# Batch 0 in tiles of 128 queries, k in the layout of q, v in one set of loads, and a new order, in a fused cosine-attention and highway kernel

## The chip, the core and the metric

The kernel runs on one core of a Trainium2 chip. A core has five engines that run side by side and meet at semaphores: TensorE (PE; its weight loads are listed as PEld), VectorE (DVE), ScalarE (ACT), GpSimd (POOL) and SyncE (SP), and 16 DMA engines. DMAs that SP and ACT issue go through hardware queues; those of POOL go through a software queue and can change the type on the way (fp32 to fp16 here). The metric is the device time of one execution in microseconds; lower is better. The kernel before took 270.19 us (median of three runs, 269.24 to 270.47).

## What is computed

```python
# q, k, v: (8, 12, 448, 64) fp32: batch, heads, sequence, head dimension; tau = 0.1
q_n = q / (norm(q) + 1e-6);  k_n = k / (norm(k) + 1e-6)
scores = q_n @ k_n.T / tau                     # no mask
attn = softmax(scores);  y = attn @ v
x = y.transpose(0, 2, 1, 3).reshape(3584, 768) # heads side by side
H = relu(x @ w_h);  T = sigmoid(x @ w_t + b_t) # w_h, w_t: (768, 768)
out = T * H + (1 - T) * x                      # (3584, 768) fp32
```

So each of the 8 batches has an attention of 12 heads, and then a highway layer over its 448 rows; here the latter is called the FFN.

## The kernel before, in words

**Tiling.** A row of the sequence is l * 7 + j, with l from 0 to 63 and j from 0 to 6. Heads are taken in three *quads* (g = 0, 1, 2) of four heads, two *pairs* each (s = 0, 1); pair p of batch b has number n = 6b + p. The two heads of a pair (t = 0, 1) lie in the upper and lower half of TensorE's rows. q has partition (s, l) and 7 x 64 values of a row set; it is normalised to `qn`, turned by seven transposes a quad into `Tq` and copied to `qT`. k has another layout before: 384 of the 448 keys as three chunks of 128 (`kr`, or for batch 0 fp32 pieces in the `os` buffers), the last 64 keys of each head apart as *tails* (`kt`, with a block-diagonal `kb`). v is split in the same way (`vr`, `vt`, and `vp`, which holds it with a column of ones).

**Steps of a batch.** Squares of q and k on ACT (`norm_q`, `norm_k`, `norm_t`: lines L368, L388, L391, L402), sums on DVE (L376, L397, L404), the reciprocal root by two Newton steps in seven short DVE instructions (`newton`, L416 to L423), scaling on POOL (`scale_q` L434, `scale_k` L495, `scale_kb` L502; for the first quad partly on DVE), transposes on PE (L446, L460, L465) and copies out of PSUM on DVE (L451, L471 to L475). For each pair then six score matmuls in three row-paired groups (`scores`, L531) and one for the tails (L542), 448 queries wide, each followed by an exp on ACT (L537, L544): seven exps a pair. `attend` makes the product with v (L556, L561, L569), a reciprocal (L576) and the scaling into `x` (L577). `ffn(b, i)` has four tiles a batch (i = 0 to 2 with two j each, i = 3 with the last): transposes of x (L600), a copy (L602), products with `wt` and `wh` (L616, L613), `za` adds the bias (L625), tanh on ACT (L632), `gt`, `hm`, `gg` on DVE (L634, L628, L637), `out` on POOL or DVE (L642), and the store `st` on SP. `x` of a batch is one token: FFN tile 0 of batch 0 waits for all six pairs.

**Order.** No loop sets the order. Every step is registered as an operation with a sequence number (`pl.op`), and the tuple `ORDER` lists these numbers in the order in which they are emitted; each engine and each DMA queue works through its own in that order. `SLOTS` gives each use of a ring (a set of buffers) its buffer. `PORT` names the kinds of DVE and POOL operations between which an ordering wait is added. 18 matmuls on zeros (`wm`, L279) run first on PE.

**The start.** SP loads quad 0 of q (448 KB) and ACT the first sixth of k (192 KB), SP then the tails, the other sixths, the other quads. POOL clears `vp` (L266), loads v in halves, then k and v of batch 1 (L309, L327), later `wt` and `wh` (L335). The bias comes on SP behind q of batch 2.

Of the kernel before, what the change touches and what calls it, by code (L numbers as in the profile page):

```python
# [8 lines left out]
FP32 = mybir.dt.float32  # L9
# [120 lines left out]
}  # L130


PORT = ("nt", "gt", "gg", "vc", "qn", "kn", "kb", "vt", "out")


class Op:
# [65 lines left out]
def kernel(  # L202
# [11 lines left out]
    nc = tc.nc  # L214
# [555 lines left out]
```

## Time and profile before

| | us |
|---|---|
| median of three runs | 270.19 |
| the profiled execution | 270.06 |
| its span, first to last instruction | 268.3 |
| PE busy | 251.6 |
| DVE busy | 233.4 |
| ACT busy | 214.5 |
| POOL busy | 169.8 |

The 1.76 us between the execution's time and its span lie outside the instructions. A view by windows gives, for each stretch, the busy time of each engine with its number of instructions, the clock that TensorE was granted (1.00 is full speed), the mean share of the DMA engines' time (over 1 where transfers overlap on one engine) and the rate. A row of the timeline or of the chain of waits begins with its start and its length in us. In a row of groups, the number after "x" is the count, then come busy time and the mean length in ns. Matmuls overlap in the pipeline and their ends are modelled, so that a "busy" PE can still be held up by a producer: how much PE does is read from counts.

### The profile page before, as it was taken

How to read it: one execution, taken by the hardware profiler on the slowest of the kernel's cores; microseconds unless marked ns; L12 is line 12 of the kernel's file. 1: busy time of each engine (PE TensorE's matmuls, PEld its weight loads, DVE VectorE, ACT ScalarE, POOL GpSimd, SP SyncE). 2: the span in 40 equal slices, each digit the busy share in tenths (PEclk: the TensorE clock that was granted, in tenths of full speed). 3: DMA queues.
4: the chain of work that ended last, by engine and by line, in shares of the span. 5: the costliest groups of instructions: out<-in, count | busy, mean ns of one | idle time of the engine just before them, and what ended most of it. 6: DMA issues, size and time to landing. Idle time of an engine off the chain costs nothing.

```text
span 268.3 us, 7687 instructions
## 1 busy us (share of the span) xinstructions
PE 251.6 (94%) x3042; PEld 158.8 (59%) x3042; DVE 233.4 (87%) x523; ACT 214.5 (80%) x421; POOL 169.8 (63%) x212
## 2 busy tenths in 40 slices
PE   8375999999999999999999999999999999999990
PEld 2122566656756576657656685666666675667660
DVE  2987988799999999999989899999998788657993
ACT  3389899999589997999899996999979757883120
POOL 6467878306975679668957397659555686320650
PEclk9755799999999999999999999999999999999998
DMA  7999999999307990496995972990513101052146
GB/s 173 298 290 181 208 270 261 213 255 126 44 18 221 234 182 14 146 257 159 151 142 185 164 107 67 330 135 4 147 23 100 29 15 49 0 147 65 29 135 190
DMA packets 51092, 38.64 MB, mean 144 GB/s; under 512 B 37488, under 2 KB 47856, under 8 KB 51056
## 3 DMA queue, kind: packets, MB, share of 16 engines
q1 hardware_dynamic: 25888, 26.75, 36.2%
q0 software_dynamic: 24896, 11.21, 33.1%
q8 instruction: 24, 0.39, 0.5%
q10 hardware_dynamic: 272, 0.20, 0.2%
q14 instruction: 12, 0.10, 0.1%
HBM read 38.34 MB, written 11.01 MB: 184 GB/s over the span
## 4 chain that ended last, share of the span: by engine, by line
PE 81%; DMA 6%; DVE 4%; ACT 4%; SPq 1%; issue 1%; POOL 1%; ACTq 0%; DVEq 0%
PE B L616 33%; PE B L531 12%; PE B L561 10%; PE B L613 5%; DMA os<-in_k_dram 4%; PE B L556 4%; PE B L600 4%; PE B L446 3%; PE B L542 3%; PE B L569 3%; PE B L460 3%; ACT E L537 3%; DMA out_dram<-os 1%; PE B L465 1%; DVE hm L628 1%
## 5 line engine op out<-in xcount | busy, mean ns | idle before, releaser
L537 ACT ACTIVATE E<-B 128x448 f16<-128x448 f32 x288 | 137.4, 577 | 15.6 <-PE B L531 12.6
L642 POOL TENSOR_TENSOR os<-x,hm 128x384 f32<-128x384 f16 x53 | 47.5, 911 | 50.2 <-DVE hm L637 39.6
L616 PEld LDWEIGHTS <-xT 128*128 128x128 f16 x576 | 51.2, 98 | 34.8 <-issue 7.5
L434 POOL TENSOR_TENSOR qn<-qr,y 128x448 f16<-128x448 f32 x47 | 43.4, 934 | 24.6 <-issue 8.1
L616 PE MATMUL B<-wh,xT 128*128 128x384 f16 x288 | 57.6, 326 | 0.0
L616 PE MATMUL B<-wt,xT 128*128 128x384 f16 x288 | 56.7, 326 | 0.0
L531 PE MATMUL B<-qT,kT 64*128 64x448 f16 x288 | 43.5, 367 | 2.8 <-DVE kT L473 1.5
L561 PE MATMUL B<-vp,E 128*128 128x65 f16 x864 | 44.5, 195 | 0.0
L561 PEld LDWEIGHTS <-E 128*128 128x128 f16 x864 | 39.1, 99 | 2.9
L632 ACT ACTIVATE tt<-z 128x768 f16<-128x768 f32 (+1 forms) x32 | 25.3, 793 | 18.5 <-DVE z L625 14.8
L495 POOL TENSOR_TENSOR kp<-kr,y 128x384 f16<-128x384 f16 x42 | 34.3, 827 | 8.2 <-DVE tt L634 2.6
L628 DVE SCALAR_TENSOR_TENSOR hm<-B,x 128x384 f16<-128x384 f32 x56 | 30.5, 549 | 3.0 <-PE B L616 1.7
L556 PE MATMUL B<-vp,Et 128*128 128x130 f16 x144 | 32.3, 224 | 0.0
L625 DVE TENSOR_TENSOR z<-B,bias 128x384 f32<-128x384 f32 x48 | 25.9, 551 | 6.5 <-PE B L616 5.5
L544 ACT ACTIVATE Et<-B 128x448 f16<-128x448 f32 x48 | 27.9, 597 | 3.1 <-PE B L542 2.8
L577 DVE SCALAR_TENSOR_TENSOR x<-B,rd 128x448 f16<-128x448 f32 x48 | 29.2, 617 | 0.6
L376 DVE TENSOR_REDUCE n<-sq 128x14 f32<-128x896 f32 (+1 forms) x25 | 25.8, 1040 | 1.2 <-ACT sq L368 1.2
L397 DVE TENSOR_REDUCE n<-sq 128x18 f32<-128x1152 f32 (+2 forms) x17 | 21.5, 1269 | 4.2 <-ACT sq L388 3.8
L368 ACT ACTIVATE sq<-qr 128x896 f32<-128x896 f32 (+1 forms) x24 | 23.1, 978 | 1.1 <-DMA qr<-in_q_dram 1.1
L531 PEld LDWEIGHTS <-kT 64*128 64x128 f16 x288 | 10.3, 94 | 20.1 <-issue 12.3
L556 PEld LDWEIGHTS <-Et 128*128 128x128 f16 x144 | 14.1, 98 | 7.9 <-issue 4.7
L542 PE MATMUL B<-qT,kT 128*128 128x448 f16 x48 | 17.4, 371 | 1.1 <-DVE kT L475 1.1
(59 smaller groups left out, 363.3 us busy)
## 6 DMA issues: line engine op xcount, KB each, us to landing
qr<-in_q_dram SPq DMA_DIRECT2D x7, 1344.0 KB, 7.6
out_dram<-os SPq DMA_DIRECT2D x48, 192.0 KB, 3.3
kr<-in_k_dram POOLq DMA_DIRECT2D x7, 576.0 KB, 12.2
vr<-in_v_dram POOLq DMA_DIRECT2D x7, 576.0 KB, 10.3
kt<-in_k_dram SPq DMA_DIRECT2D x16, 96.0 KB, 6.4
vt<-in_v_dram SPq DMA_DIRECT2D x16, 96.0 KB, 7.5
out_dram<-os SPq DMA_DIRECT2D x16, 96.0 KB, 2.9
qr<-in_q_dram SPq DMA_DIRECT2D x3, 448.0 KB, 6.9
```

The costliest lines, as they stand in the source:

```text
L434: ENG[eng].tensor_mul(R("qn", 3 * b + g)[:, :, t, :], R("qr", b)[:, g + 3 * t, :].rearrange("l (j d) -> l j d", d=D), R("y", b)[:, c : c + ...
L495: ENG[eng].tensor_mul(R("kp", 6 * b + p).rearrange("l c t d -> l t c d"), a, kcol(b, p))
L531: nc.tensor.matmul(R("B", ("S", n, c, t))[:, 0:S], lhsT=R("kT", i)[ln, s, 128 * c : 128 * c + 128], rhs=R("qT", i)[ln, s, :], start=True, ...
L537: nc.scalar.activation(R("E", n)[:, at : at + 7, :].rearrange("l j x -> l (j x)"), R("B", ("S", n, c, t))[:, 0:S], AF.Exp)
L544: op("ACT", f"expt {n}", lambda: nc.scalar.activation(R("Et", n).rearrange("l j x -> l (j x)"), R("B", ("St", n))[:, 0:S], AF.Exp), r=[("B ...
L556: nc.tensor.matmul(U[:, 2 * c : 2 * c + 2, :], lhsT=Et[:, 2 * c : 2 * c + 2, :].rearrange("l j x -> l (j x)"), rhs=vp[:, 6:8, 0:65], start ...
L561: nc.tensor.matmul(U[:, 2 * c + t, :], lhsT=E[:, at : at + 2, :].rearrange("l j x -> l (j x)"), rhs=vp[:, 3 * t + m, 0:65], start=False, s ...
L577: op("DVE", f"ev {n}", lambda: nc.vector.scalar_tensor_tensor(out=R("x", b)[:, :, D * p : D * p + D], in0=U_()[:, :, 0:D], scalar=0.0, in1 ...
L616: nc.tensor.matmul(P[:, 0:MH], lhsT=xT[:, cc, :], rhs=w_[:, cc, MH * mh : MH * mh + MH], start=(cc == 0), stop=(cc == CC - 1))
L625: op("DVE", f"za {g} {mh}", lambda at=at, sl=sl: nc.vector.tensor_add(R("z", g)[:, sl], R("B", at)[:, 0:MH], biast[:, :] if tail else bias ...
L628: op("DVE", f"hm {g} {mh}", lambda at=at, sl=sl, mh=mh: nc.vector.scalar_tensor_tensor(out=R("hm", g)[:, sl], in0=R("B", at)[:, 0:MH], sca ...
L642: op(eng, f"out {g} {mh}", lambda sl=sl, mh=mh: ENG[eng].tensor_add(R("os", g)[:, sl], xpart(mh), R("hm", g)[:, sl]), r=[("gg", g), ("x", ...
```

## The change

The queries of batch 0 are worked in four tiles like those of the FFN: `attend0(g, i)` does, for quad g, 128 queries (64 for i = 3), writes `x` as tokens `("x", 0, i)`, and FFN tile i of batch 0 needs only its own. Its scores are 128 (64) columns wide, the tails' scores share a bank with those of t = 0, and one exp of 512 and one of 384 columns do what seven of 448 did for a quarter of the queries. Batches 1 to 7 keep `scores` and `attend`.

k takes the layout of q, for all batches: one load, squares and sums of 896 columns a quad, `kn` with eight slots of two heads (the first and last half zero), eight transposes a quad, one copy. The tails' loads, squares, sums and scalings go. k of batch 0 comes in fp32 by hardware queues, a quad at a time, into the `E` buffers; it must be scaled before exps can use the buffer. v comes in four loads a batch on POOL, its tails among them; SP's loads of tails go. The Newton steps of batch 0 are replaced by ln and exp on ACT (`lnexp`), which need another activation table: one is loaded at the start, and a second one (`table2`) after the last `lnexp`. The clearing of `vp` moves from POOL to DVE, ahead of the zeros for the matmuls. Loads of q for batches 1 and up are *held* on SP until the ACT instruction ahead of them in the order has ended. qT and kT have four buffers instead of three, xT five instead of three.

With the numbers of the new `ORDER` resolved to operations, the queues begin as follows (batch, quad, half):

```
SP   q 0 0; k 0 1; q 0 1; q 0 2; k 0 2; (held) q 1 0; q 1 1; q 1 2; bias; (held) q 2; q 3; st 1; ...
POOL load k 1; ident; four loads v 0; load wt; load wh; kn 0 0 1; qn 0 0 1; load k 2; qn 0 1; kn 0 1; kn 0 2 1; qn 0 2; ...
ACT  load k 0 0; table; sq q 0 0 (one half); sq k 0 0 (two halves); ln, exp; sq k 0 1; sq q 0 1; sq q 0 2; ln, exp;
     sq k 0 2; two exps; sq k 1 0; ln; exp tile; exp; three exps; sq q 1 0; table2; 20 exps, 18 of them of tiles 0 and 1; ...
DVE  vp; zeros; ... sq q 0 0 (other half); four sums; kn 0 0 0; qn 0 0 0; sum k 0 1; zeros of kn 0; sum q 0 1; copy kT 0; copy qT 0; ...
PE   18 x wm; turn k 0 0; turn q 0 0; scores of quad 0, tiles 0 and 1; turn q 0 1; turn k 0 1; ...
```

On PE, the FFN of batch 0 stands among the scores and products of batch 0's tiles 1 to 3 and of batch 1. As before, its last part (tile 3) and the last product of batch 1 (pair 11) stand right ahead of the turn of q of batch 2.

The diff, cut:

```diff
-    WARM = 18
+    WARM, NF = 18, 0
+    XDMA = ()
+    GROUPS = ((0, 1), (1, 2), (2, 3)), ((0, 1), (1, 3)), ((0, 3),)
+    LG = ((0, 0), (0, 28), (0, 56))
+    SCALE = {("q", 0, 0): ("DVE", "POOL"), ("k", 0, 0): ("DVE", "POOL")}
...
+        self.held = eng == "SP" and kind == "ldq" and name.split()[1] != "0"
...
+    def ld_kf(g, eng):
+        op(eng, f"ldf {g}", lambda: ENG[eng].dma_start(kf(g), q_src(k, 0)[:, :, g::3, :]), w=[("E", ("f", g))])
+    def ld_v(b):
+        for t, jj, j0, n in ((0, 0, 0, 4), (0, 1, 4, 3), (1, 0, 0, 3), (1, 1, 3, 4)):
+            def fn(t=t, jj=jj, j0=j0, n=n):
+                c = 64 if (t, jj) == (0, 1) else 0
+                nc.gpsimd.dma_start(R("vr", b)[64 * jj : 64 * jj + 64, 6 * t : 6 * t + 6, c : c + 64 * n].rearrange("l h (c d) -> l h c d", c=n),
+                                    v_src(b)[:, 6 * t : 6 * t + 6, j0 : j0 + n, :])
+            op("POOL", f"ldv{n} {b} {t} {jj}", fn, w=[("vr", b, t, jj)])
...
+    def lnexp(b, lo, hi, parts):
+        i = (b, lo)
+        op("ACT", f"ln{hi - lo} {b} {lo}", lambda: nc.scalar.activation(
+            R("tu", i)[:, 0, lo:hi], R("n2", b)[:, lo:hi], AF.Ln, bias=eps[:, 0:1]), ...
+        op("ACT", f"ie{hi - lo} {b} {lo}", lambda: nc.scalar.activation(
+            R("y", b)[:, lo:hi], R("tu", i)[:, 0, lo:hi], AF.Exp, scale=-0.5), ...
...
+    def turn(nm, b, g):
+        nj = NJ if nm == "q" else 8
+        def fn():
+            T = R16(at)[:, 0 : 128 * nj].rearrange("p (s j l) -> p j s l", s=2, j=nj)
+            for j in range(nj):
+                to = j if nm == "q" else 2 * ((j - 1) % 3) + (j - 1) // 3 if 0 < j < 7 else 6 + (j == 7)
+                nc.tensor.transpose(T[:, to], R(nm + "n", i)[:, j].rearrange("l t d -> l (t d)"), ident[:, :])
...
+    def attend0(g, i):
+        w = 128 if i < 3 else 64
+        for ss in ((0,), (1,)) if i < 3 else ((0, 1),):
+            def fq(ss=ss, A=A, B_=B_, o=o):
+                for s in ss:
+                    for c in range(NC):
+                        for t in range(2):
+                            ln, at = slice(64 * t, 64 * t + 64), unit(s)[0][t][c] - o - 512 * t
+                            nc.tensor.matmul(R("B", (A, B_)[t])[:, at : at + w], lhsT=k_()[ln, s, 128 * c : 128 * c + 128],
+                                             rhs=q_()[ln, s, 128 * i : 128 * i + w], start=True, stop=True)
...
+            for t, X, m in ((0, A, 512), (1, B_, 384)):
+                op("ACT", f"ex{m} {n}", lambda X=X, m=m, t=t, o=o: nc.scalar.activation(
+                    flat()[:, o + 512 * t : o + 512 * t + m], R("B", X)[:, 0:m], AF.Exp), ...
...
+        xk = ("x", b) if b else ("x", b, i)
...
+    op("ACT", "table2", lambda: table(0), r=[("lg", i) for i in LG], w=[("t0",)])
...
+                elif o.held:
+                    behind(made[0], act)
```

More of the change, by code (lines that the diff above doesn't have):

```diff
@@ L122 @@
[L122 to L128 removed]
+    "tu": "01010101010",
@@ L144, in __init__ @@
         kind = name.split()[0].rstrip("0123456789")
-        self.port = eng in ("DVE", "POOL") and (kind in PORT or kind == "sqq")
+        self.held = eng == "SP" and kind == "ldq" and name.split()[1] != "0"
+        self.port = eng in ("DVE", "POOL") and (kind in PORT or kind == "sq")
 class Plan:
@@ L247 @@
     biast = sb.tile([128, MH], FP32, name="biast")
-    tab = sb.tile([128, 1], FP32, name="tab")
+    eps = sb.tile([128, 1], FP32, name="eps")
     wz = sb.tile([128, 640], FP16, name="wz")
@@ L267, in zero, with table @@
         return fn
-    op("ACT", "table", lambda: nc.scalar.activation(tab[:1, :], nc.const_aps.tensor(0.0, [1, 1]), AF.Exp), w=[("tab",)])
+    def table(n):
+        return nc.scalar.add_instruction(mybir.InstLoadActFuncSet(
+            name=nc.get_next_instruction_name(), engine=nc.scalar.engine, act_func_set_id=n))
+    op("ACT", "table", lambda: table(6), w=[("t6",)])
     op("POOL", "ident", lambda: make_identity(nc, ident), w=[("id",)])
     for i, t in enumerate(TILES["vp"]):
-        op("POOL", f"zvp {i}", zero("POOL", [(t[:, :, 0:6, D : D + 1], 1.0), (t[:, :, 6:8, 0 : D + 1], 0.0),
+        op("DVE", f"zvp {i}", zero("DVE", [(t[:, :, 0:6, D : D + 1], 1.0), (t[:, :, 6:8, 0 : D + 1], 0.0),
                                     (t[0:64, :, 6, D : D + 1], 1.0), (t[64:128, :, 7, D : D + 1], 1.0)]), w=[("zvp",)])
-    for i, t in enumerate(TILES["kb"]):
-        op("DVE", f"zkb {i}", zero("DVE", [(t[0:64, :, 1, :], 0.0), (t[64:128, :, 0, :], 0.0)]), w=[("zkb",)])
-    op("DVE", "zw", zero("DVE", [(wz[:, :], 0.0)]), w=[("wz",)])
+    for i, t in enumerate(TILES["kn"]):
+        op("DVE", f"zkn {i}", zero("DVE", [(t[:, 0, 1, :], 0.0), (t[:, 7, 0, :], 0.0)]), w=[("zkn",)])
+    op("DVE", "zw", zero("DVE", [(wz[:, :], 0.0), (eps[:, :], 1e-14)]), w=[("wz",), ("eps",)])
     for i in range(WARM):
@@ new lines, with source, token, norm @@
+    SQV = ()
+    SPLIT = {("q", 0, 0): ("ACT", "DVE"), ("k", 0, 0): ("ACT", "ACT")}
+    def source(nm, b, g):
+        return kf(g) if nm == "k" and b == 0 else R(nm + "r", b)[:, g::3, :]
+    def token(nm, b, g):
+        return ("E", ("f", g)) if nm == "k" and b == 0 else (nm + "r", b, g)
+    def norm(nm, b, g):
+        i = (nm, b, g)
+        sc = tau if nm == "q" else 1.0
+        engs = SPLIT.get(i, (("DVE" if i in SQV else "ACT"),))
+        n = 3 - len(engs)
+        for t, eng in enumerate(engs):
+            ts = slice(t, t + n)
+            def fn(eng=eng, ts=ts):
+                src = source(nm, b, g)[:, ts]
+                dst = R("sq", i).rearrange("l (t x) -> l t x", t=2)[:, ts]
@@ L700 @@
-        scale_kb(b, "POOL")
-        if b == 0:
-            copy_v(b, 0, 3)
-            copy_v(b, 3, 6)
-        else:
-            copy_v(b, 0, 6)
-        cast_vt(b, "POOL")
-        for g in range(NG):
-            first = b == 0 and g == 0
-            scale_q(b, g, ("DVE", "POOL") if first else ("POOL", "POOL"))
-            for s in range(2):
-                scale_k(b, 2 * g + s, "DVE" if first else "POOL")
-            turn_q(b, g, 2 if first else 1)
-            turn_k(b, g)
-        for p in range(NP):
-            scores(b, p)
-            attend(b, p)
+        if b < 2:
+            for g in range(NG):
+                ld_qk("q", b, [g])
+                if b == 0:
+                    ld_kf(g, "SP" if g else "ACT")
+            if b:
+                ld_qk("k", b)
+            ld_v(b)
+            if b == 0:
+                ld_w(moe_w_t, wt, "wt")
+                ld_w(moe_w_h, wh, "wh")
+                ld_b()
+        else:
+            ld_qk("q", b)
+            ld_qk("k", b)
+            ld_v(b)
@@ new lines @@
+        for g in range(NG):
+            for nm in "qk":
+                norm(nm, b, g)
+        for g0, g1 in GROUPS[min(b, 2)]:
+            (lnexp if (b, 28 * g0) in LG else newton)(b, 28 * g0, 28 * g1, [(nm, g) for g in range(g0, g1) for nm in "qk"])
+        for p0 in (0, 3) if b == 0 else (0,):
+            copy_v(b, p0, p0 + (3 if b == 0 else 6))
+        copy_vt(b, "POOL")
+        for g in range(NG):
+            for nm in "qk":
+                scale(nm, b, g, SCALE.get((nm, b, g), ("POOL", "POOL")))
+                turn(nm, b, g)
@@ L717, with behind @@
+        if b == 0:
+            for i in range(4):
+                for g in range(NG):
+                    attend0(g, i)
+        else:
+            for p in range(NP):
+                scores(b, p)
+                attend(b, p)
         for i in range(4):
             ffn(b, i)
+    def behind(a, b):
+        tc.add_manual_dep(a, b.name, mybir.DependencyInfo(mybir.DependencyClass.Sync, mybir.DependencyReason.SCHED_ONLY),
+                          reason="order")
     with nc.allow_low_precision(reason="fp16 operands of the products and gates as given"):
@@ L721 @@
         with tc.manual_schedule():
-            before = None
+            before = act = None
             for o in pl.ordered(ORDER, SLOTS):
@@ L725 @@
                 o.fn()
-                if o.port:
-                    made = [i for i in nc.cur_bb.bb.instructions[made:] if i.engine == ENG[o.eng].engine]
-                    if o.eng == "DVE":
-                        before = made[-1]
-                    elif before is not None:
-                        tc.add_manual_dep(made[0], before.name, mybir.DependencyInfo(
-                            mybir.DependencyClass.Sync, mybir.DependencyReason.SCHED_ONLY), reason="port")
-                        before = None
+                made = [i for i in nc.cur_bb.bb.instructions[made:] if i.engine == ENG[o.eng].engine]
+                if o.eng == "ACT":
+                    act = made[-1]
+                elif o.held:
+                    behind(made[0], act)
+                elif o.port and o.eng == "DVE":
+                    before = made[-1]
+                elif o.port and before is not None:
+                    behind(made[0], before)
+                    before = None
 _INS = ['q', 'k', 'v', 'tau', 'moe_w_h', 'moe_w_t', 'moe_b_t']
```

393 lines of the change are left out of this document (160 added, 233 removed), and 145 rows, old and new, of the table ORDER.

## The prediction, made before the changed kernel ran

> **What bounds the kernel now.** I read the windows by stage first.
>
> ```profile
> span 268.3 us, 7687 instructions
> ...
> 16.00:20.00 4.00, 3.69 (x16) 0.84 (x12) 3.29 (x8) 4.00 (x10) 2.13 (x3) 0.50 1.29 242
> 20.00:30.00 10.00, 7.17 (x56) 3.97 (x56) 8.15 (x23) 9.20 (x17) 8.39 (x11) 0.50 1.43 185
> 30.00:40.00 10.00, 9.84 (x151) 6.23 (x148) 8.80 (x27) 9.66 (x22) 7.38 (x9) 0.97 1.13 252
> 40.00:50.00 10.00, 9.86 (x149) 6.63 (x146) 8.35 (x20) 10.00 (x23) 8.04 (x10) 1.00 1.26 237
> 50.00:60.00 10.00, 10.00 (x98) 5.66 (x95) 8.24 (x16) 10.00 (x21) 0.00 (x0) 1.00 1.34 251
> ...
> 64.00:68.00 4.00, 4.00 (x61) 2.74 (x57) 3.83 (x13) 3.75 (x8) 1.83 (x3) 1.00 1.26 147
> 68.00:71.00 3.00, 3.00 (x61) 2.13 (x58) 2.98 (x9) 1.53 (x2) 3.00 (x5) 1.00 0.05 5
> 71.00:75.00 4.00, 4.00 (x49) 2.76 (x48) 4.00 (x9) 1.59 (x3) 3.85 (x6) 1.00 0.22 49
> ...
> 60.00:262.00 202.00, 201.87 (x2554) 131.72 (x2552) 184.00 (x396) 165.40 (x324) 133.65 (x158) 1.00 0.55 114
> ```
>
> Columns: PE, PEld, DVE, ACT, POOL, PE's clock, DMA share, GB/s. The reader is to see two regimes. From 16 to 68 us ACT is full (46.6 of the 48 us that are shown); from there on PE is, and ACT falls back at once to half (3.1 of 7 us from 68 to 75). PE's column alone would hide the first regime: it says "busy" from 30 us on. The chain of waits (first a part of it from 0 to 90 us, then the summary of 60 to 90) and ACT's timeline date the change of regime.
>
> ```profile
> 16.86 2.80 ACT E L537 x7
> ...
> 43.93 1.00 PE B L600 x18
> ...
> 45.86 2.06 PE B L616 x12
> ...
> 70.92 0.50 PE B L446 x7
> ...
> by line: PE B L616 45.0%; PE B L531 12.7%; PE B L561 10.7%; PE B L613 6.5%; PE B L600 4.5%; PE B L446 4.3%; PE B L542 4.1%; PE B L556 4.0%; PE B L569 3.7%; PE B L460 3.7%; PE B L465 1.1%
> ```
>
> ```profile
> 66.26 0.54 ACT L544 ACTIVATE Et<-B 128x448 f16<-128x448 f32 x1 [0.25 <-PE B L542]
> ...
> 74.66 2.73 ACT L537 ACTIVATE E<-B 128x448 f16<-128x448 f32 x6 [1.75 <-PE B L531]
> ```
>
> The exps begin at 16.86 us. The FFN of batch 0 can begin only when all six pairs are through: its first transposes stand at 43.93, its first products at 45.86. ACT ends the last exp of batch 1 at 66.26 + 0.54 = 66.80. PE reaches the turn of batch 2's first q at 70.92, 4.1 us later, with nothing but PE in the chain from 60 us on, and ACT then waits for PE's new scores until 74.66. So PE comes out of the start 4.1 us behind ACT, because its FFN work, which needs no exp, came late. **The milestone** is this turn: in both orders the same work lies ahead of it (attention of batches 0 and 1, FFN of batch 0), and I take what is gained there as gained at the end, since PE sets the pace behind it. After the change it cannot stand before ACT's last exp of batch 1 and the product behind it.
>
> **The start.** All that moves the first exp.
>
> ```profile
> 1.26 1.24 POOL L266 MEMSET vp<- 128x36 f16 x4
> ...
> 1.26 1.28 ACT L388 ACT_TABLE_LOAD   x1 [1.26 <-PEq L751]
> ...
> 5.57 0.52 ACT L388 ACTIVATE sq<-os 128x384 f32<-128x384 f32 x1 [3.03 <-DMA os<-in_k_dram]
> ...
> 8.30 0.18 DVE L416 TENSOR_SCALAR y<-n 128x20 int32<-128x20 int32 x1
> ...
> 9.52 0.19 ACT L269 ACTIVATE tab<-const-float32-0.0 1x1 f32<-1x1 f32 x1
> ...
> 9.92 0.18 DVE L423 SCALAR_TENSOR_TENSOR y<-tu,y 128x20 f32<-128x20 f32 x1
> ...
> 14.83 0.56 PE L531 MATMUL B<-qT,kT 64*128 64x448 f16 x2 [1.50 <-DVE kT L473]
> ```
>
> ```profile
> 0.00:12.00 12.00, 6.75 (x18) 2.33 (x18) 6.78 (x22) 4.66 (x8) 6.34 (x18) 0.92 0.94 230
> ```
>
> ```profile
> L368 ACT ACTIVATE sq<-qr 128x896 f32<-128x896 f32 x23 | 22.5, 996 | 1.1 <-DMA qr<-in_q_dram 1.1
> ...
> L376 DVE TENSOR_REDUCE n<-sq 128x14 f32<-128x896 f32 x23 | 24.7, 1077 | 1.2 <-ACT sq L368 1.2
> ...
> L471 DVE COPY kT<-B 128x1024 f16<-128x1024 f16 x21 | 14.3, 681 | 0.7 <-PE B L465 0.7
> ```
>
> The first k comes as 448 KB, not 192: 256 KB more at 230 GB/s is 1.1 us, so the squares begin near 6.7 instead of 5.57. The last of four half sums on DVE (0.54 each, half of 1077 ns, behind one half square of about 0.6) ends near 9.5. Newton took from 8.30 to 10.10, 1.8 us; ln and exp are two small ACT instructions, bounded by the 0.19 of a one-element exp below and, with hand-overs, 0.6 in all: y at 10.0. Then DVE does two scalings (0.6 each), and by the new order also a sum of k's second quad (1.08) and the zeros of `kn` (0.2) before the turn of k may start: 12.5. Eight transposes at half clock take 0.9, while DVE sums q's second quad to 13.6; the copies of k (0.68) and q (0.62) end at 14.9. So the first scores stand where they stood (14.83), and the first exp at 16.0 to 16.8, as ACT's last squares of batch 0 come ahead of it in both orders. I take 16.0, a gain of 0.9. The clearing of `vp` delays the zeros on PE by up to 1.24 us, which only brings them closer to the first turn: nothing.
>
> **ACT from there to the milestone.** Before it took 66.80 - 16.86 = 49.9 us, of which 46.6 of 48 busy in the rows above, so some 1.4 idle. The counts stay: 84 exps (42 of them as 512 and 384 columns, two for two of 448), squares of two batches of 2688 columns of k and as many of q, two tanhs. New are the second table load (1.28, the row of the first) and ln and exp of the last quad (0.4): 1.7. With half the idle time left, 49.9 + 1.7 - 0.7 = 50.9: last exp at 66.9. Behind it comes one product of a pair, whose price is in this row of the chain:
>
> ```profile
> 68.60 0.37 PE B L569 x14
> ```
>
> with three groups of about 0.25 before it: 1.2 us. Milestone at 68.1 instead of 70.92: **2.8 us gained**, if PE has no backlog by then. In the new order the first product of FFN tile 0 stands behind scores whose PSUM banks come free with the 26th exp: 3.7 us of squares, ln and table and 26 exps at 0.40 (2.80 for seven) after 16.0 are 30.1, with copies between near 31 instead of 45.86. To lose a backlog of 4.1 us PE then has 15 us more in which everything else on it goes at ACT's pace. Had it no spare time there, the milestone would stand where it was; that is a bound, and part of a rival below.
>
> The Trainium skill, "ScalarE: Activation LUTs", section "What ACT_TABLE_LOAD costs", gives the same 1283 ns for the load, but adds a drain of 1380 ns on a switch. The first load here has nothing to drain, so no row shows it; by the page 1.4 us of the 2.8 would remain.
>
> **Other edits.** The scores of batch 0 become 54 row-paired groups of 128 columns and 18 of 64 in place of 18 of 448.
>
> ```profile
> 80.34 0.67 PE B L531 x6
> ```
>
> By columns they cost the same (0.223 a group before, 4.0 in all); if the halves don't overlap, two at 0.056 (18 transposes in 1.00) for each group of 128 and two of half that for 64, 7.1. So 0 to 3.1 us, nearest to the columns' price, as both rows are row-paired forms of one instruction: 1, under ACT's regime and so hidden; it costs that 1 if PE has the backlog after all.
>
> ```profile
> L495 POOL TENSOR_TENSOR kp<-kr,y 128x384 f16<-128x384 f16 x42 | 34.3, 827 | 8.2 <-DVE tt L634 2.6 <-PE B L531 1.6 <-PE B L446 1.5
> ...
> L502 POOL TENSOR_TENSOR kb<-kt,y 64x384 f16<-64x384 f32 x16 | 13.6, 852 | 3.0 <-DVE y L423 1.8 <-DVE vp L509 0.6
> ...
> L327 POOL DMA_DIRECT2D vr<-in_v_dram x7 | 7.5, 1070 | 0.0
> ...
> L331 POOL DMA_DIRECT2D vr<-in_v_dram x4 | 3.2, 806 | 0.0
> ```
>
> POOL, a batch: scaling of k six at 965 ns (827 by 448/384) in place of six at 827 and two at 852, -0.9; v's loads four at 0.81 for one of 1.07, +2.2: 1.3 more, 9 in all, on an engine with 133.65 of 202 us busy. Nothing, unless a late scaling holds a turn: up to 1 us. On ACT and DVE the k columns of a batch stay (2688), so nothing; transposes a quad stay eight; SP loses 32 loads of tails. The held loads of q: behind a held load stand the bias and the stores.
>
> ```profile
> bias<-in_moe_b_t_dram SPq DMA_DIRECT2D x1, 384.0 KB, 16.3
> ...
> wt<-in_moe_w_t_dram POOLq DMA_DIRECT2D x1, 1152.0 KB, 20.3
> ```
>
> The bias follows the third load of q of batch 1, held to near 23. Before it stood behind a load of 1344 KB and took 16.3 us; now it stands behind 448, so between half of that and all: 31 to 39, and the FFN's first addition wants it at 32. `wt` is issued near 8 instead of 17: 28 with the 20.3 it took. Both are just in time; late by 5 us, they would eat a third of the 15 us: nothing in the sum, 2 at worst.
>
> Sum: 268.3 - 2.8 = 265.5, plus 1.76 outside: 267.3; the median shown lies 0.1 above the profiled 270.06, so **267.4 us**. Its own range is 265.7 (no idle time, first exp at 15.0) to 269.9 (all idle time, first exp at 16.8, 1 for the small scores).
>
> **Rivals.**
> *Contention at the start (slower).* POOL now issues k of batch 1, v and the weights within 8 us, where before 12 us it issued little; they meet batch 0's own q and k on the same DMA engines. If these get half of the 230 GB/s, the two quads of q and k that the copies of quad 0 stand behind (1.84 MB) need 16.0 us, then come 1.0 and 1.08 for square and sum and 1.3 for the copies: first scores at 19.4, exps at 20.5. With all of the idle time, 20.5 + 51.6 + 1.2 = 73.3 for the milestone, 2.4 later: 272.5. It decides from a first exp past 18.8 (70.92 - 1.2 - 50.9). For: a DMA share of 0.94 already in the first 12 us. Against: shares of 1.24 to 1.43 from 16 to 68 us show that transfers of two queues overlap on an engine, so that the hardware's part need not halve. The Trainium skill, "DMA: Bandwidth & Descriptors", section "Queues, rings and completion order", has each engine go round the queues that have work, packet by packet, which is this half; no row of before has both queues full in the first 12 us.
> *No change.* First exp at 17.5 by a milder contention and ACT's idle time back (waits for q of batch 1, whose squares stand ahead of 60 exps): 17.5 + 51.6 + 1.2 = 70.3, 0.6 gained: 269.6.
> *Larger gain.* DVE is as full as PE behind 68 us (6.98 of 7), and batch 0's additions and maxima there move ahead of 60 us, where DVE has slack.
>
> ```profile
> L628 DVE SCALAR_TENSOR_TENSOR hm<-B,x 128x384 f16<-128x384 f32 x56 | 30.5, 549 | 3.0 <-PE B L616 1.7 <-ACT E L537 0.4 <-PE B L613 0.2
> ...
> L625 DVE TENSOR_TENSOR z<-B,bias x5: 541/558/558, 47.2 to 56.4; 128x384 f32<-128x384 f32 x5
> ```
>
> Five of seven additions ran before 60 us; two more and five maxima at 0.55 are 3.9 us off a stretch where DVE may set the pace: 267.4 - 3.9 = 263.5. Against: the chain there has no DVE.
>
> **How the numbers follow.** Forecast 0.40, contention 0.20, no change 0.17, larger gain 0.23. 0.5% (1.35 us) is about what a measurement of this kernel tells from no change. Faster by that, below 268.84: 0.23, most of the forecast's 0.40 (0.34) and little else: 0.58. Slower, above 271.5: contention and a bad end of the rest, 0.22. The rest 0.20. The range, 262.5 to 273.0, leaves out the worst of contention and a tenth of the larger gain.
>
> **What would show it.** Right: first exp at 16 to 16.8, FFN's first product near 31, no gap on ACT until a last exp of batch 1 at 67, the turn of batch 2's q within 2 us of it, 197 us from there to the end as before. Wrong: a first exp past 18; gaps on ACT that end with q of batch 1 or with a DVE stuck on the bias; a turn of batch 2 that stands early while the end does not move.

## The result, and the profile after

| | before | after |
|---|---|---|
| median us (lowest to highest) | 270.33 (269.24 to 271.25, four runs) | 267.02 (266.67 to 267.67, four runs) |
| ratio, with its 95% interval | | 0.9882 (0.9838 to 0.9926) |
| the profiled execution | 270.06 | 266.69 |
| its span | 268.3 | 264.5 |
| outside the span | 1.76 | 2.19 |

The changed kernel is faster by 1.2%, and the interval lies wholly below 1. The forecast was 267.4. I read the views in the order in which the prediction used them: the page's line of busy times, then the windows of the changed kernel (columns as before).

```profile
PE 249.6 (94%) x3168; PEld 162.8 (62%) x3168; DVE 225.1 (85%) x510; ACT 215.7 (82%) x425; POOL 169.4 (64%) x210
```

```profile
0.00:12.00 12.00, 7.38 (x25) 3.00 (x26) 8.12 (x25) 5.02 (x8) 7.58 (x15) 0.98 0.92 252
...
20.00:30.00 10.00, 9.15 (x150) 7.56 (x150) 7.58 (x24) 9.32 (x20) 6.74 (x10) 0.75 1.13 254
30.00:40.00 10.00, 9.80 (x169) 7.04 (x165) 9.35 (x19) 10.00 (x21) 2.75 (x4) 1.00 1.26 222
40.00:50.00 10.00, 9.83 (x127) 5.87 (x126) 8.45 (x25) 10.00 (x21) 6.65 (x9) 1.00 0.99 210
50.00:60.00 10.00, 9.91 (x141) 6.45 (x139) 9.67 (x22) 10.00 (x21) 8.35 (x11) 1.00 1.08 238
...
67.20:71.20 4.00, 3.58 (x40) 2.22 (x39) 3.93 (x8) 3.36 (x6) 3.86 (x5) 1.00 0.07 9
...
67.08:264.50 197.42, 190.48 (x2391) 124.13 (x2385) 170.65 (x377) 157.35 (x311) 126.25 (x152) 0.99 0.49 109
```

The last of these windows runs from the milestone to the end. The same window of the kernel before is:

```profile
70.86:268.30 197.44, 191.08 (x2387) 124.30 (x2385) 175.97 (x377) 156.37 (x309) 125.42 (x149) 0.99 0.54 117
```

The sums of PE, ACT and POOL differ by at most 2.0 us, that of DVE is 8.3 less; what differs is where the work lies. ACT is full from 30 to 60 us (before 9.66, 10.00 and 10.00). PE does more from 20 to 30 us, 9.15 instead of 7.17. In the 4 us behind the milestone ACT falls back less (3.36 of 4 busy, where it was 1.59), but what it does there is squares: its next exp starts at 70.31, 3.2 us behind the turn, and before at 74.66, 3.8 behind it. From the milestone to the end DVE has 5.3 us less to do (170.65 against 175.97).

The timeline of ACT, then that of PE, date the same points as before:

```profile
5.59 0.58 ACT L377 ACTIVATE sq<-qr 128x448 f32<-128x448 f32 x1 [3.06 <-DMA qr<-in_q_dram]
...
8.83 0.23 ACT L414 ACTIVATE y<-tu 128x28 f32<-128x28 f32 x1
...
14.43 0.95 ACT L377 ACTIVATE sq<-E 128x896 f32<-128x896 f32 x1 [0.85 <-DMA E<-in_k_dram]
15.28 0.96 ACT L563 ACTIVATE E<-B 128x384 f16<-128x384 f32 x2
...
18.99 0.98 ACT L377 ACTIVATE sq<-qr 128x896 f32<-128x896 f32 x1
19.99 1.28 ACT L282 ACT_TABLE_LOAD   x1
21.28 3.76 ACT L563 ACTIVATE E<-B 128x384 f16<-128x384 f32 x8
25.66 5.34 ACT L563 ACTIVATE E<-B 128x384 f16<-128x384 f32 x12 [0.62 <-PE B L550]
30.75 1.08 ACT L377 ACTIVATE sq<-qr 128x896 f32<-128x896 f32 x1
...
39.25 2.06 ACT L563 ACTIVATE E<-B 128x384 f16<-128x384 f32 x4
...
61.77 4.29 ACT L479 ACTIVATE E<-B 128x448 f16<-128x448 f32 x9
70.31 1.85 ACT L479 ACTIVATE E<-B 128x448 f16<-128x448 f32 x4 [0.64 <-PE B L473]
```

```profile
11.34 1.00 PE L442 MATMUL B<-ident,kn 128*128 128x128 f16 x8 [2.04 <-POOL kn L425]
...
31.90 1.15 PE L657 MATMUL B<-wt,xT 128*128 128x384 f16 x6
...
66.96 0.20 PE L511 MATMUL B<-vp,Et 128*64 128x65 f16 x2
67.08 0.56 PE L442 MATMUL B<-ident,qn 128*128 128x128 f16 x7
```

The prediction took 16.86, 43.93, 45.86 and 70.92 from the chain, which counts an instruction from the end of the one before it on its engine. I compare like with like, so here is the kernel before by its timeline (first transposes and first products of the FFN, then the turn); its first exp stands there at 16.77.

```profile
43.77 1.17 PE L600 MATMUL B<-ident,x 128*128 128x128 f16 x18
...
45.79 2.12 PE L616 MATMUL B<-wt,xT 128*128 128x384 f16 x12
...
70.86 0.56 PE L446 MATMUL B<-ident,qn 128*128 128x128 f16 x7
```

The first exp stands at 15.28 (before 16.77), the FFN's first product at 31.90 (45.79), the last exp of batch 1 ends at 61.77 + 4.29 = 66.06 (66.80), and the turn of batch 2's first q, the milestone, stands at 67.08 (70.86). That is 3.78 us earlier, and they reach the end whole: from the milestone to the end of the span are 264.5 - 67.08 = 197.4 us, and before 268.3 - 70.86 = 197.4.

The gain has two parts. The last exp of batch 1 ends 0.74 earlier. The other 3.04 lie between it and the turn: 4.06 us before (70.86 - 66.80), 1.02 now. Now only the products of pair 11 stand there (the row ahead of the turn is their end); before there were also most of those of pair 9 and the end of batch 0's FFN (the rest of tile 2 and all of tile 3), which PE had not reached.

### The profile page after: what moved, and what is told of

It reads as the page before. It is cut to its first block, busy times and chain, and to the rows that moved or that the text cites. A ratio compares the mean times of both kernels' runs of the same rounds, so it can differ in the third digit from the quotient of the medians.

```text
span 264.5 us, 7894 instructions
## 1 busy us (share of the span) xinstructions
PE 249.6 (94%) x3168; PEld 162.8 (62%) x3168; DVE 225.1 (85%) x510; ACT 215.7 (82%) x425; POOL 169.4 (64%) x210
## 4 chain that ended last, share of the span: by engine, by line
PE 83%; ACT 6%; DMA 4%; DVE 2%; issue 2%; SPq 1%; DVEq 0%
PE B L657 35%; PE B L473 11%; PE B L503 9%; PE B L442 7%; PE B L654 5%; DMA E<-in_k_dram 4%; PE B L633 4%; PE B L498 4%; ACT E L563 3%; PE B L484 3%; PE B L511 3%; ACT sq L377 2%; ACT E L479 1%; PE B L577 1%; PE B L550 1%
## 5 line engine op out<-in xcount | busy, mean ns | idle before, releaser
L479 ACT ACTIVATE E<-B 128x448 f16<-128x448 f32 x252 | 121.6, 595 | 16.1 <-PE B L473 13.0
L385 DVE TENSOR_REDUCE n<-sq 128x14 f32<-128x896 f32 (+1 forms) x50 | 51.3, 1037 | 1.6 <-ACT sq L377 1.6
L425 POOL TENSOR_TENSOR kn<-kr,y 128x448 f16<-128x448 f16 x42 | 38.9, 935 | 20.6 <-DVE y L403 13.6
L503 PE MATMUL B<-vp,E 128*128 128x65 f16 x756 | 38.5, 193 | 0.0
L503 PEld LDWEIGHTS <-E 128*128 128x128 f16 x756 | 33.7, 98 | 2.3
L473 PE MATMUL B<-qT,kT 64*128 64x448 f16 x252 | 34.4, 354 | 0.0
L335 POOL DMA_DIRECT2D vr<-in_v_dram x32 | 21.7, 683 | 0.0
L377 ACT ACTIVATE sq<-kr 128x896 f32<-128x896 f16 x21 | 21.6, 1029 | 0.0
L563 ACT ACTIVATE E<-B 128x384 f16<-128x384 f32 (+1 forms) x42 | 20.6, 629 | 0.7 <-PE B L550 0.6
L643 DVE COPY xT<-B 128x768 f16<-128x768 f16 (+1 forms) x32 | 15.7, 497 | 4.4 <-PE B L633 4.1
```

Of the source, the lines that this page charges most:

```text
L377: nc.scalar.activation(dst, src, AF.Square, scale=sc)
L385: nc.vector.reduce_sum(R("n2", b)[:, c : c + 7 * n], a, axis=AX.X)
L425: ENG[eng].tensor_mul(R(nm + "n", i)[:, o : o + NJ, t, :], source(nm, b, g)[:, t].rearrange("l (j d) -> l j d", d=D), R("y", b)[:, c : c + ...
L473: nc.tensor.matmul(R("B", ("S", n, c, t))[:, 0:S], lhsT=R("kT", i)[ln, s, 128 * c : 128 * c + 128], rhs=R("qT", i)[ln, s, :], start=True, ...
L479: nc.scalar.activation(R("E", n)[:, at : at + 7, :].rearrange("l j x -> l (j x)"), R("B", ("S", n, c, t))[:, 0:S], AF.Exp)
L503: nc.tensor.matmul(U[:, 2 * c + t, :], lhsT=E[:, at : at + 2, :].rearrange("l j x -> l (j x)"), rhs=vp[:, 3 * t + m, 0:65], start=False, s ...
```

## The experiments

All start from the changed kernel unless said otherwise; where an edit changes the order, the numbers in `ORDER` change with it. Every ratio is to the kernel before, run in turn with it on the same chip. The last four columns come from the profiled execution: the end of the last exp of batch 1, the milestone, the span, and what lies between the last two. The sessions ran on different chips, and the kernel before had medians from 269.37 to 270.37 in them; so kernels of different rows are better compared by ratio, milestone and span than by their medians.

| kernel | median us | ratio (95% interval) | last exp | milestone | span | to the end |
|---|---|---|---|---|---|---|
| before | 270.33 | 1 | 66.80 | 70.86 | 268.3 | 197.4 |
| after | 267.02 | 0.9882 (0.9838 to 0.9926) | 66.06 | 67.08 | 264.5 | 197.4 |
| a_tables | 269.34 | 0.9963 (0.9939 to 0.9987) | 68.97 | 69.99 | 267.5 | 197.5 |
| b_tables (from before) | 272.90 | 1.0096 (1.0064 to 1.0129) | 68.78 | 72.84 | 270.5 | 197.7 |
| a_ffnlate | 287.66 | 1.0645 (1.0610 to 1.0680) | 85.91 | 87.13 | 285.5 | 198.4 |
| a_resched | 271.04 | 1.0060 (1.0039 to 1.0081) | 69.56 | 70.62 | 268.7 | 198.1 |
| a_ffnlate2 | 280.78 | 1.0418 (1.0398 to 1.0439) | 80.48 | 81.51 | 279.1 | 197.6 |
| a_rings | 266.53 | 0.9861 (0.9825 to 0.9896) | 66.16 | 67.18 | 264.7 | 197.5 |
| a_newton | 270.26 | 1.0025 (1.0009 to 1.0041) | 69.55 | 70.59 | 268.4 | 197.8 |
| a_pool4 | 267.61 | 0.9932 (0.9912 to 0.9952) | 66.99 | 68.01 | 265.6 | 197.6 |
| a_tlate | 267.51 | 0.9910 (0.9878 to 0.9942) | 66.42 | 67.44 | 264.9 | 197.5 |
| a_pool4_tlate | 267.77 | 0.9913 (0.9884 to 0.9943) | 66.89 | 67.91 | 265.5 | 197.6 |
| a_relief | 267.90 | 0.9935 (0.9909 to 0.9961) | 67.65 | 68.68 | 266.3 | 197.6 |
| a_pool2_tlate | 266.82 | 0.9901 (0.9865 to 0.9937) | 66.32 | 67.35 | 264.9 | 197.5 |

Two columns carry the reading. The time from the milestone to the end stays within 1 us, whatever happens ahead of it (0.7 without the one kernel whose milestone moved by 20): the milestone is the right place to measure. And the turn follows the last exp by 1.0 to 1.2 us in every kernel that has the changed kernel's operations, by 4.1 in the two that have those of before. The two kernels with a late FFN (`a_ffnlate` 1.2, `a_ffnlate2` 1.0) are among the former: there the FFN's work stands ahead of the last exp and makes that later. So the 3.04 above tells what stood behind the last exp in these two orders; it is no measure of the early FFN by itself.

**Does ACT set the pace?** Two more loads of activation tables (1.28 us each) lengthen ACT at 20 us and touch nothing else, once in the changed kernel and once in the one before.

```diff
-    op("ACT", "table2", lambda: table(0), ...
+    op("ACT", "table2", lambda: [table(n) for n in (0, 6, 0)][-1], ...
```

> The changed kernel with two more activation-table loads right at its second one: 2 x 1.28 us more on ACT near 20 us, nothing else. If ACT sets the pace of the changed kernel up to the last exp of batch 1 and PE carries that to the end, all 2.6 us show: 269.6 us (269.0 to 270.2), with the last exp of batch 1 near 68.4 instead of 65.8. If PE or DVE already sets the pace there, at most 0.6 shows: 267.0 to 267.6.

```diff
+    op("ACT", "tables", lambda: [table(n) for n in (6, 0)])      # before: placed in ORDER ahead of an exp of pair 1
```

> The kernel before with the same two table loads on ACT at the same point of time (between two exps of pair 1). If PE there runs 4.1 us behind ACT at the turn of batch 2, that backlog takes up most of the 2.6 us: 270.3 to 271.5 us. If ACT sets the pace in this kernel too, it is 272.9.

ACT's and PE's timelines, first of the changed kernel with more loads, then of the kernel before with them (there L605 transposes x and L451 is the turn of q):

```profile
20.05 3.86 ACT L282 ACT_TABLE_LOAD   x3
...
64.68 4.29 ACT L479 ACTIVATE E<-B 128x448 f16<-128x448 f32 x9
...
69.99 0.56 PE L442 MATMUL B<-ident,qn 128*128 128x128 f16 x7
```

```profile
20.05 2.57 ACT L271 ACT_TABLE_LOAD   x2
...
45.75 1.17 PE L605 MATMUL B<-ident,x 128*128 128x128 f16 x18
...
72.84 0.56 PE L451 MATMUL B<-ident,qn 128*128 128x128 f16 x7
```

In the changed kernel 2.57 us of loads move the milestone by 2.91 and the span by 3.0: ACT's start sets the pace, as expected. In the kernel before they move it by 1.98, and the median is 272.90, where the expectation had 272.9 if ACT sets the pace there too. That answers a question on the prediction's "backlog": had PE been 4.1 us behind by itself, it would have absorbed a delay of ACT. It doesn't, since the FFN of batch 0 waits for the last x of batch 0, which hangs on ACT: its first transposes stand at 45.75 instead of 43.77, 1.98 later, and the milestone 1.98 later. Behind that point PE is full (27 us from 43.77 to 70.86). So before the change the path was ACT up to x of batch 0, then PE with the whole of that FFN still to do.

**What does the early FFN do?** The FFN tiles of batch 0 wait again for all of batch 0's x:

```diff
-        xk = ("x", b) if b else ("x", b, i)
+        xk = ("x", b) if b else ("x", b, "all")      # attend0 writes ("x", 0, "all")
```

> The changed kernel with only this undone: the FFN of batch 0 waits for all of batch 0's x (all quads, all tiles), and its operations are put one by one between the others from there on, near 50 us. Batch 0 stays in tiles, the start and the loads stay. If the early FFN is what gains, PE has some 8 us more to do between 50 and 66 us and comes out 4 to 6 us behind: 271 to 273 us. If the gain is from the start or from the order behind batch 1, it stays at 267.0 to 267.8.

It missed by far. The FFN's operations were put into the order one by one behind it, so that each engine's queue stood behind operations that weren't ready: from 60 to 80 us the exps of batch 1 wait up to 4.34 us for their scores. That measures the order as much as the dependence. So the next pair takes both orders from one list scheduler.

> The changed kernel with the operations between the first transposes of FFN tile 0 and the turn of batch 2's first q put in another order, by a list scheduler that gives each engine the next listed operation that is ready; nothing else differs. It is the control for the next kernel, whose order comes from the same scheduler. My theory (ACT sets the pace up to the last exp of batch 1, the products behind it are few): 266.5 to 269.0, turn of batch 2's q between 66.5 and 69.5. If the gain of the change lay in the particular order and not in what it allows, it goes: 270 or more.

> The control before this one with one dependence put back as it was before the change: the FFN tiles of batch 0 wait for x of all of batch 0 (all 24 products of its tiles) instead of their own tile's; order of that stretch again by the list scheduler. Theory 'the early FFN is what lets PE end with ACT': FFN of batch 0 begins near 43 as before the change, PE has its work left over when ACT's last exp of batch 1 is through, turn of batch 2's q 4 to 7 us later than in the control, 270.5 to 274. Rival 'the gain is the earlier first exp and nothing else' (0.5 to 1.6 us of the 3.8): no more than 1.5 us over the control, below 269.

The control itself lost 4.0 us to the changed kernel (271.04 against 267.02) and is slower than the kernel before (ratio 1.0060): "266.5 to 269.0" is missed, and by the expectation's own rule (270 or more) the gain hangs on the particular order: what the change allows brings nothing in this one. Behind the last exp it leaves as little as the changed kernel (1.06 us); what it lost is the last exp itself, at 69.56 instead of 66.06. With the FFN late it is 9.7 us slower again (280.78 against 271.04), where 4 to 7 at the milestone was expected. PE's timeline and windows of that kernel:

```profile
49.99 1.04 PE L442 MATMUL B<-ident,kn 128*128 128x128 f16 x8 [4.18 <-ACT E L563]
...
81.51 0.56 PE L442 MATMUL B<-ident,qn 128*128 128x128 f16 x7
```

```profile
40.00:50.00 10.00, 3.81 (x42) 1.61 (x41) 5.34 (x16) 8.27 (x18) 5.88 (x9) 0.55 1.39 205
```

PE has no FFN work to put between the products and scores of 40 to 50 us: 3.81 busy of 10, one wait of 4.18 for an exp, and its clock falls to 0.55. The FFN's first product comes at 56.83, and the milestone 10.9 later than in the control. The rival that only the earlier first exp counts (at most 1.5 us) falls. The size, 9.7, doesn't carry over: the FFN's first transposes, which wait for x of batch 0, stand at 55.61 here and stood at 43.77 before the change. So that a late FFN costs is shown; how much of the gain the early one brings is not.

**Buffers.** `a_rings` gives qT and kT three buffers instead of four and xT three instead of five, in the same order.

> The changed kernel with three buffers again for qT, kT and xT (four, four and five in the change), in the same order. If the gain is all made by the turn of batch 2, nothing: 266.7 to 267.6. If the additional buffers let the stretch behind it run faster, 1 us or more is lost: 268.2 and up.

266.53, just below the range for "nothing", with a milestone at 67.18: nothing is lost. The added buffers may go.

**Ln and exp in place of Newton.** `a_newton` goes back to Newton's steps for batch 0 (`LG = ()`, one table with exp and tanh from the start, no second load).

> The changed kernel with the reciprocal roots of batch 0 again by Newton steps on DVE in place of ln and exp on ACT; the second table load (1.28 us on ACT) and six small ACT instructions go, DVE gets three times seven short ones. Theory 'ACT sets the pace': the first exp comes 1.0 to 1.5 us later (Newton 1.8 us in place of 0.6), ACT has 2.5 to 2.9 us less to do behind it, the net is a gain of 1 to 1.9 at the last exp of batch 1 if nothing else is late, so 265.1 to 266.9. Rival 'the start decides': 1.0 to 1.5 us slower than the changed kernel, 268 to 268.5. Rival 'no pace is set by ACT's table load because PE is the bound from 45 on': within 0.3 of the changed kernel.

All three were too low: 270.26, 3.2 us above the changed kernel (3.5 at the milestone). Rows of ACT, DVE and POOL in it:

```profile
20.34 0.98 ACT L563 ACTIVATE E<-B 128x384 f16<-128x384 f32 x2 [2.36 <-POOL kn L425]
...
15.57 0.19 DVE L403 SCALAR_TENSOR_TENSOR y<-tu,y 128x28 f32<-128x28 f32 x1
...
19.10 0.19 DVE L403 SCALAR_TENSOR_TENSOR y<-tu,y 128x28 f32<-128x28 f32 x1
...
19.37 2.73 POOL L425 TENSOR_TENSOR kn<-E,y 128x448 f16<-128x448 f32 x3 [1.70 <-DVE y L403]
```

The first exp comes no later at all (15.07): it stands behind ACT's square of k's third quad, which waits for its load in both kernels (it starts at 14.21 here, at 14.43 in the changed kernel). The loss lies with quads 1 and 2. Each Newton is seven steps on DVE that follow each other by 0.22, and sums of 1.05 and copies of 0.6 stand between and ahead of them; so y of quad 1 is ready at 15.76 and that of quad 2 at 19.29, against 13.58 and 17.78 with ln and exp. POOL's scalings follow, and ACT waits for them. So the ln and exp of the change pay for the second table load more than twice over, and not where the prediction looked for it.

**Can ACT be relieved?** Four squares go from ACT to POOL, which has 10.4 us without work there:

```diff
+    SQP = (('k', 1, 2), ('k', 1, 1), ('k', 2, 2), ('k', 2, 0))
-        engs = SPLIT.get(i, (("DVE" if i in SQV else "ACT"),))
+        engs = SPLIT.get(i, (("POOL" if i in SQP else "DVE" if i in SQV else "ACT"),))
```

> The changed kernel with four squares (k quads 1 and 2 of batch 1, k quads 0 and 2 of batch 2; 0.85 us each on ACT) moved from ACT to POOL, which has 10.4 us without work from 32.8 to 43.2 us; a square of 896 columns on POOL is estimated at 1.9 us from the scaling of 448 columns in 0.935. Theory 'ACT sets the pace up to the last exp of batch 1': 3.4 us less on ACT, up to 3.4 earlier at the turn of batch 2's q, less what PE has to do behind ACT: 263.3 to 265.5. Rival 'PE is the bound from 45 us on': within 0.5 of the changed kernel. A square that comes late on POOL would hold the next batch's turn and show as a wait of DVE's sums for POOL.

No gain: 267.61, with the milestone 0.93 later. Rows of ACT, POOL, DVE and PE in it (its line numbers are 3 higher), and DVE's row of the same step in the changed kernel:

```profile
38.28 0.98 ACT L482 ACTIVATE E<-B 128x448 f16<-128x448 f32 x2 [1.04 <-PE B L476]
...
38.85 3.32 POOL L380 TENSOR_TENSOR sq<-kr 128x896 f32<-128x896 f16 x2 [2.81 <-DMA kr<-in_k_dram]
...
40.97 1.27 DVE L402 TENSOR_TENSOR tu<-y 128x56 f32<-128x56 f32 x1
...
42.88 1.62 PE L660 MATMUL B<-wh,xT 128*128 128x384 f16 x9 [0.82 <-DVE x L587]
```

```profile
40.56 0.21 DVE L399 TENSOR_TENSOR tu<-y 128x56 f32<-128x56 f32 x1
```

Two things took it. ACT comes earlier and then waits for scores (1.04 at 38.28): PE is full too from 30 to 41 us and doesn't move. And a Newton step on DVE took 1.27 us instead of 0.21: it ends at 42.24, when POOL's second square ends (38.85 + 3.32 = 42.17). x behind it on DVE's queue was late, and PE with it.

The next three move the second table load behind the exps of 20 to 40 us, alone, with the squares on POOL, and with one more square on DVE (`SQV = (("q", 1, 0),)`).

> The changed kernel with the second table load moved on ACT from 20 us to right ahead of the first tanh (about 41 us); nothing else is moved. Theory 'both are full': ACT sets the pace up to about 31 us, behind that PE and ACT are both full up to the last exp of batch 1. Then 1.28 us is won at 20 us and given back at 41: last exp and turn of batch 2's q within 0.5 of the changed kernel, 266.5 to 267.5. Rival 'from 31 us on PE alone sets the pace': ACT has room at 41, the 1.28 is kept, 265.6 to 266.0.

> The same move of the second table load in the kernel that has four squares on POOL, where ACT stood without work for 3.1 us between 30 and 50 us. Theory 'both are full': relieving ACT behind 31 us gained nothing since PE was full too; now 1.28 us is taken off the stretch in which ACT sets the pace, and ACT has the room to take the load at 41: 0.8 to 1.3 below the kernel with four squares on POOL, ratio to the kernel before 0.988 to 0.991. Rival 'ACT does not set the pace ahead of 31 us either': within 0.3 of it.

> The same again, and the square of q's first quad of batch 1 (0.98 us on ACT at 19 us) on DVE, which has 2.2 of 4 us without work from 16 to 20 us. Theory 'ACT sets the pace up to 31 us': another 0.3 to 0.9 (POOL's scaling of k's third quad, at 21.9 us, holds the turn behind it and takes part of it): ratio to the kernel before 0.982 to 0.988. Rival: POOL or DVE becomes the bound of the start, no gain over the kernel with the load alone moved.

ACT's timeline of the first:

```profile
21.98 7.96 ACT L563 ACTIVATE E<-B 128x384 f16<-128x384 f32 x18 [0.99 <-POOL kn L425]
29.61 1.16 ACT L377 ACTIVATE sq<-qr 128x896 f32<-128x896 f32 x1
...
38.33 1.92 ACT L563 ACTIVATE E<-B 128x384 f16<-128x384 f32 x4
40.27 1.28 ACT L282 ACT_TABLE_LOAD   x1
```

The first came out as "both full" had it: 267.51 by the median, milestone 0.36 later. With the load gone from 20 us ACT waits 0.99 for POOL's scaling of k's third quad (row at 21.98), but no longer 0.62 for PE at 25.66, and the square that stands at 30.75 in the changed kernel stands at 29.61: 1.14 of the 1.28 are won. Of these 0.92 are left at the last exps ahead of the load (38.33 against 39.25); then the 1.28 are paid, and the difference, 0.36, is what the last exp and the milestone are later. In the second kernel less is won at the start: ACT waits 0.90 for POOL and 0.67 for PE, and the same square stands at 30.50 instead of 30.94. So the 0.8 to 1.3 expected of it didn't come (0.16 above the kernel without the move by the medians, 0.1 below by the spans, a ratio of 0.9913 against 0.9932 with intervals that overlap), and its rival, "ACT does not set the pace ahead of 31 us either", holds there: ACT, POOL and PE wait for each other by turns, so that lengthening ACT costs in full while shortening it gains a part. The third, at 0.9935 where 0.982 to 0.988 was expected, points the same way: the square took 1.81 us on DVE and pushed back sums and scalings, ACT waits 2.15 for POOL at 23.12, and the milestone is 0.77 later than in the second.

The last takes only the two squares that lie beside no Newton step, and the late load:

> The changed kernel with the second table load moved to ahead of the first tanh and only the two squares of k's quads 1 and 2 of batch 1 on POOL (31 to 36 us); those of batch 2, beside which a DVE instruction of 0.21 took 1.27 us and held PE's queue, stay on ACT. Theory 'behind 31 us PE is as full as ACT, and the loss of the kernel with four squares came from that stall': the loss is gone, turn of batch 2's q 0.2 to 0.8 earlier than in the changed kernel (66.3 to 66.9), 266.2 to 266.9, ratio to the kernel before 0.984 to 0.988. Rival 'ACT alone sets the pace behind 31 us': 1.7 us less on ACT come through, turn at 65.3 to 65.7, 265.3 to 265.7. Rival 'squares on POOL cost as much wherever they stand': turn at 67.5 or later, 267.5 or more.

```profile
37.43 0.98 ACT L482 ACTIVATE E<-B 128x448 f16<-128x448 f32 x2 [1.04 <-PE B L476]
...
40.17 1.28 ACT L282 ACT_TABLE_LOAD   x1
...
67.35 0.56 PE L445 MATMUL B<-ident,qn 128*128 128x128 f16 x7
```

266.82, the milestone at 67.35: the median falls in the theory's range, the ratio (0.9901) and the milestone just past it, by 0.45 us, and neither differs from the changed kernel's by what can be measured. The stall on DVE is gone (the step takes 0.20), and the rival that squares on POOL cost as much anywhere (a turn at 67.5 or later) falls, if narrowly. ACT gives what it had won by 37 us to a wait for PE, and behind 41 us, where it is full to the last exp, the load counts whole. No version beats the changed kernel beyond what the runs can tell.

## Why the prediction came out, step by step

**The milestone and the path.** The two regimes and the choice of the milestone were right: 197 us to its end were forecast, and 197.4 stand in both profiles. The "4.1 us behind ACT" were right as a length and loose as a cause: `b_tables` shows no slack of PE, but FFN work that could only begin behind x of batch 0. At the hand-over itself the changed kernel's chain of waits leaves PE for DVE (`hm`, `x`, `rd`, `x`, from 66.20 to 68.14), and PE, just past the turn, stands 0.42 for that x.

**The start.** First exp forecast at 16.0, measured 15.28. One step that was off is the landing of the larger k: 5.1 us after its issue, before 4.8 for 192 KB, so 0.3 and not the 1.1 forecast.

```profile
E<-in_k_dram ACTq DMA_DIRECT2D x1, 448.0 KB, 5.1
```

```profile
os<-in_k_dram ACTq DMA_DIRECT2D x1, 192.0 KB, 4.8
```

The 230 GB/s that priced it are a mean over 12 us in whose first two next to nothing moves; between 3 and 4 us it is 371. So k's squares begin at 6.07 instead of 6.7, y is there at 9.06 instead of 10.0, the turn of k begins at 11.34 instead of 12.5 and the first scores at 13.92 instead of 14.83. But the first exp waited for none of these: ahead of it on ACT stands the square of k's third quad, and that waited 0.85 for its load (row at 14.43). The prediction put this square ahead of the first exp, but its sum gave the load of it no time. The chain of the changed kernel begins with it:

```profile
3.05 11.36 DMA E<-in_k_dram
```

**ACT to the last exp.** Forecast 50.9 us from first to last exp, measured 66.06 - 15.28 = 50.78. The sum was right, and the 1.28 of the second load is nearly all felt: without it ACT is 1.14 earlier at 30 us (`a_tlate`). The drain behind a switch of 1.38 us, cited from the Trainium skill, "ScalarE: Activation LUTs", section "What ACT_TABLE_LOAD costs", is not seen: the square ahead of the load ends at 19.97, the load takes 19.99 to 21.27, the next exp begins at 21.28.

**Behind the last exp.** Forecast 1.2, measured 1.02; the FFN's first product near 31, measured 31.90. Both hold, and the sum comes out: 1.0 us of milestone better than forecast (0.7 at the first exp, the rest in the two steps behind it), 0.4 given back outside the span (2.19 against 1.76), and 0.2 by the median, which lies 0.33 above the profiled execution where 0.1 was taken. So that the forecast is only 0.4 off is partly luck: 3.8 us of span were gained, not 2.8. The profiled runs of the other kernels have 1.8 to 2.6 us there, so that the 0.4 is no effect of the change.

**Edits at nothing.** The small scores:

```profile
30.84 0.44 PE B L550 x12
```

This row of the chain gives 0.073 for a group of 128 columns, near the columns' price as taken (0.223 x 128/448 = 0.064) and far from 0.112. The group of k's scalings on POOL:

```profile
L425 POOL TENSOR_TENSOR kn<-kr,y 128x448 f16<-128x448 f16 x42 | 38.9, 935 | 20.6 <-DVE y L403 13.6 <-DVE vp L451 4.4 <-DVE hm L678 2.1
```

Scalings of 0.935 (0.965 forecast) and v loads of 0.683 (0.81) leave POOL where it was, 169.4 us busy. The bias is issued at 22.70 and lands 9.6 later, at 32.3, within the forecast's 31 to 39, and the first addition stands at 34.95: in time.

**The rivals.** *Contention*: the first exp was to pass 18.8; it came at 15.28, and the first q landed 4.8 us after its issue, before 4.5. (The DMA shares that the prediction set against this rival run from 1.13 to 1.43 in its rows, not from 1.24.) The Trainium skill, "DMA: Bandwidth & Descriptors", section "Queues, rings and completion order", has each engine go round its queues, packet by packet. Here batch 0's first loads lost at most 0.3 us that way; the third k took 11.36 for the same 448 KB and held the first exp, and what POOL's loads have to do with that no run tests. *No change* needed a first exp at 17.5 and ACT's idle time back; neither is there. *Larger gain*: DVE was relieved by 5.3 us behind the milestone, more than the 3.9 counted, and that stretch kept its 197.4. DVE, though full there, is not what ends last.

**What stays open.** What part of the 3.78 us the earlier start of the FFN alone would bring in the order of before: no kernel tried that without a new order, and the new order is worth as much (the control lost 4.0 us). What the first exp would gain from an earlier third load of k is open too. PE's clock had a share that was not forecast and not tested (below).

## What to carry to other kernels

Where one engine is full first and another after it, look for work of the second that waits on a token coarser than it needs; cutting that token (here x of a batch into tiles) gives the second engine work to put between the first one's, and what it leaves behind the hand-over shrinks. Measure such a change at one milestone behind the hand-over, and see that the time from there to the end stays. When two or three engines come within a microsecond of each other, lengthening one costs in full and relieving one gains a part or nothing: then the order decides, and a generic scheduler can lose as much as the change brought.

## What the runs showed of the hardware

PE's clock came back to full some 5 us earlier; from 20 us on PE had denser work (9.15 of 10 against 7.17 in the windows above and of before); that the one is the reason of the other no run tests. Windows of the kernel before, then of the changed one:

```profile
25.00:30.00 5.00, 4.70 (x42) 2.59 (x42) 4.40 (x7) 4.20 (x8) 4.89 (x7) 0.50 1.40 190
```

```profile
25.00:30.00 5.00, 4.79 (x100) 3.71 (x98) 2.81 (x14) 4.38 (x12) 3.54 (x5) 0.99 1.12 261
```

A DVE instruction on two operands was held until a POOL square ended: 1.27 us instead of 0.21 in `a_pool4` and again in `a_pool4_tlate`, and 0.20 in `a_pool2_tlate`, where no square runs beside it. The Trainium skill, "GPSIMD Engine Reference", section "1. Specifications", has GpSimd's interfaces to SBUF shared with VectorE and names DVE instructions with two inputs in SBUF among those that contend. The step held here reads y twice, so the trace agrees, and adds the size: 1.06 us, to the end of POOL's instruction. A square of 896 columns on POOL took 1.68, against the estimate of 1.9.
